# Instructions of five engines, put into the program with and without a block around them

## The chip, the cores and the metric

The kernel runs on one core of one Trainium2 chip. The metric is the device time in microseconds of one execution; the time of before is the median of three runs. A core has five engines that run on their own and meet only at semaphores: TensorE (PE; its weight loads are shown apart as PEld), VectorE (DVE), ScalarE (ACT), GpSimd (POOL) and SyncE (SP), which here only issues DMAs and waits. A name with a q behind it (SPq, PEldq) is the engine's instruction queue: rows of waits, drains, branches and DMA issues.

## The reference

For a tensor x of 2048 rows of 640 values, layer-normalised to xn, the sum of three things is computed: x itself, a spectral filter of xn and a small dense network on xn.

```python
def reference(A_x, A_w_r, A_w_i, B_x, B_w1, B_b1, B_w2, B_b2):
    x = A_x
    xn = _layernorm(x, axis=-1)
    # A: rfft2 of xn, times (w_r + 1j * w_i), irfft2
    # B: gelu(xn @ w1 + b1) @ w2 + b2, with w1 640 x 1536 and w2 1536 x 640
    return x + _A_ref(xn, A_w_r, A_w_i) + _B_ref(xn, B_w1, B_b1, B_w2, B_b2)
```

All tensors are bf16. B_x is not used.

## The kernel before

The 2048 rows lie in SBUF as 16 groups of 128 rows. The Fourier transforms are matmuls with tables that the program holds as constants (G and H for the long axis, E and GE for the short one, M and N for the small inner steps), with folds and unfolds on VectorE around them. The dense network runs on TensorE beside them: the first layer in six blocks of row groups and 12 feature blocks each, with GELU on ScalarE; the second layer and the last step of the inverse transform add up in the same PSUM banks. The last addition (line 961, on VectorE) reads a PSUM bank and the sum of x and b2, and writes an output tile; SP stores it to DRAM at line 964, 18 stores in all.

The kernel doesn't call the engines in the order of the text. Each step is put down as an operation with what it reads and writes (class Sched). The table ORDER has the fixed order of operations for each engine. `schedule` gives out the buffers, `sync` works out which waits are needed, and `emit` puts the instructions into the program: for every operation of an engine, first its waits (`wait_ge`, line 434), then the instruction itself, with a semaphore increment where somebody waits for it. SP, at the end of its list, waits for all stores (`last`, line 442), so that the kernel doesn't end before its output has landed.

Three lines matter for the change. Line 989 is where the program object is made; what the program does ahead of the kernel's own first instruction (constants, a first meeting of all engines) is shown with this line in the profile. Line 428 opens a block, entered into the `ExitStack` of line 493; lines 444 to 448 give it one body for each engine. The block is closed where that `with` statement ends, and what the closing puts into the program is shown in the profile with line 493.

Of the kernel before, what the change touches and what calls it, by code (L numbers as in the profile page):

```python
# [220 lines left out]
class Sched:  # L221
# [6 lines left out]
    def op(self, engs, prio, emit, reads=(), writes=(), after=(), rows=None, gate=(), alts=None, late=0.0):  # L228
        o = Op()
        o.name = writes[0].name if writes else ""  # L230
        o.engs, o.prio, o.emit = engs, prio, emit
        o.reads, o.writes, o.after = list(reads), list(writes), list(after)
        o.gate = gate if isinstance(gate, list) else list(gate)
        o.rows, o.late = rows, late
        o.nbytes = rows is not None
        o.alts, o.alt = alts, None
        o.seq = len(self.ops)
        o.eng, o.done, o.inc, o.count, o.sem = None, False, False, None, None
        o.deps = [w for b in o.reads for w in b.writers] + list(after)
        for b in o.reads:  # L240
            b.readers.append(o)
        for b in o.writes:
            b.writers.append(o)
        self.ops.append(o)
        return o
# [171 lines left out]
    def emit(self, es, last):  # L417
        nc = self.nc
        sems = {e: nc.alloc_semaphore(f"s_{e}") for e in self.engines if e != "sp"}
        for e in self.engines:  # L420
            n = 0
            for o in self.order[e]:
                if o.nbytes:
                    o.sem, o.count = nc.alloc_semaphore(f"d_{o.seq}"), 16
                elif o.inc:
                    n += 1
                    o.sem, o.count = sems[e], n
        block = es.enter_context(nc.Block())

        def run(name):  # L430
            def go(e):
                for o in self.order[name]:
                    for d in o.waits:
                        e.wait_ge(d.sem, d.count)
                    ins = o.emit(e, name) if o.alts is None else o.emit(e, o.alt)
                    if o.nbytes:
                        ins.then_inc(o.sem, 16)
                    elif o.inc:
                        ins.then_inc(o.sem, 1)
                if name == "sp":  # L440
                    for o in last:
                        e.wait_ge(o.sem, o.count)
            return go
        block.sync(run("sp"))
        block.gpsimd(run("pool"))
        block.vector(run("dve"))
        block.scalar(run("act"))
        block.tensor(run("pe"))


BLOCKS = [(0, 2), (2, 2), (4, 2), (6, 2), (8, 4), (12, 4)]
# [552 lines left out]
```

## Time and profile before

| | us |
|---|---|
| median of 3 runs | 147.75 (147.56 to 147.98) |
| the profiled execution's own time | 148.03 |
| its span, first to last instruction | 146.1 |
| TensorE busy in it | 140.2 |
| VectorE busy | 112.7 |
| ScalarE busy | 80.9 |
| GpSimd busy | 23.7 |

The span is measured from the start of the first recorded instruction to the end of the last; the execution's own time is longer, as it also has what lies before and behind. Waits, drains, branches and DMA issues are not counted as busy. In a view by line, a row has the line, the engine's queue, the operation, a count, the shortest, median and longest duration in nanoseconds, and the first and last start in microseconds from the span's start, printed to a tenth. The granted TensorE clock is 1.0 over the whole span.

### The profile page before, as it was taken

The numbers are of one execution on the slowest core, as the hardware profiler recorded it, in microseconds if no ns is written. First come the engines' busy times: TensorE is split into PE (matmuls) and PEld (weight loads), VectorE is DVE, ScalarE is ACT, GpSimd is POOL, SyncE is SP. The second block draws the span as 40 slices with busy tenths as digits, with TensorE's granted clock in tenths as the row PEclk, the third lists the DMA queues.
The fourth block names the chain that finished last, engine by engine and source line by source line (L and its number), as shares of the span: only waits on it lengthen the run. The fifth ranks groups of instructions, "written<-read, shape, count | busy, mean of one in ns | idle before, by whom it ended". The sixth has DMA issues, their size and how long they took to land.

```text
span 146.1 us, 4081 instructions
## 1 busy us (share of the span) xinstructions
PE 140.2 (96%) x1702; PEld 90.8 (62%) x1720; DVE 112.7 (77%) x235; ACT 80.9 (55%) x145; POOL 23.7 (16%) x40
## 2 busy tenths in 40 slices
PE   7999999999999999999999999999999999999993
PEld 7788998888465455446544645554446666556572
DVE  1999999999844449789966967992422998998982
ACT  3208999999989769763555633216376755201000
POOL 2330302206100009220100120000063700000000
PEclk9999999999999999999999999999999999999999
DMA  4999999999997875949446571444559885103234
GB/s 110 320 407 354 320 132 303 150 182 241 283 162 149 193 192 123 235 99 180 94 92 121 63 154 30 40 110 94 90 116 230 175 202 180 45 4 137 90 135 135
DMA packets 30873, 23.63 MB, mean 162 GB/s; under 512 B 20488, under 2 KB 26888, under 8 KB 30728
## 3 DMA queue, kind: packets, MB, share of 16 engines
q1 hardware_dynamic: 28432, 17.81, 52.4%
q0 software_dynamic: 2368, 5.57, 17.4%
q8 instruction: 13, 0.21, 0.6%
q14 instruction: 4, 0.03, 0.1%
q10 hardware_dynamic: 56, 0.01, 0.0%
HBM read 13.55 MB, written 2.62 MB: 111 GB/s over the span
## 4 chain that ended last, share of the span: by engine, by line
PE 91%; DVE 4%; issue 2%; DMA 2%; POOL 0%
PE ps L552 90%; DVE stats L674 2%; DMA X<-in_A_x_dram 2%; DVE T L699 1%; DVE mv L676 0%; DVE xnT L564 0%; POOL rstd L678 0%; PE ps L718 0%; DVE W L961 0%
## 5 line engine op out<-in xcount | busy, mean ns | idle before, releaser
L552 PE MATMUL ps<-xnT,W 128*128 128x256 bf16 (+2 forms) x384 | 58.7, 300 | 0.2 <-DVE mv L676 0.2
L552 PE MATMUL ps<-W,gT 128*128 128x512 bf16 (+3 forms) x380 | 55.7, 292 | 1.6 <-issue 1.1
L552 PEld LDWEIGHTS ps<-W,gT 128*128 128x128 bf16 x396 | 30.3, 98 | 23.5 <-issue 1.6
L552 PEld LDWEIGHTS ps<-xnT,W 128*128 128x128 bf16 x384 | 33.3, 98 | 16.3 <-issue 1.6
L778 ACT ACTIVATE gT<-ps,b1col 128x256 bf16<-128x256 f32 (+1 forms) x72 | 35.3, 557 | 6.8 <-PE ps L552 6.5
L674 DVE BATCH_NORM_STATS2 stats<-X 128x6 f32<-128x320 bf16 x32 | 13.9, 475 | 2.2 <-DMA X<-in_A_x_dram 2.2
L563 ACT ACTIVATE Wf<-ps 128x960 bf16<-128x960 f32 (+1 forms) x8 | 7.0, 901 | 13.5 <-PE ps L552 13.5
L946 POOL DMA_DIRECT2D X<-in_A_x_dram x8 | 7.1, 1067 | 40.1 <-DMA Wf<-in_A_w_r_dram 17.6
L845 DVE TENSOR_TENSOR T<-Y,Wf 128x1288 bf16<-128x1288 bf16 x16 | 12.7, 826 | 0.0
L946 POOL DMA_DIRECT2D xnT<-in_A_x_dram x8 | 7.4, 1151 | 25.3 <-ACT xnT L928 25.3
L678 POOL TENSOR_TENSOR rstd<-mv,mhalf 128x2 f32<-128x2 f32 (+1 forms) x10 | 7.2, 715 | 26.8 <-DVE mv L676 26.7
L563 ACT ACTIVATE Xb<-ps 128x960 bf16<-128x960 f32 (+1 forms) x7 | 7.7, 1102 | 6.8 <-PE ps L552 6.8
L564 DVE CAST Y<-ps 128x644 bf16<-128x644 f32 x8 | 6.5, 828 | 5.5 <-PE ps L552 5.5
L563 ACT ACTIVATE XV<-ps 128x1280 bf16<-128x1280 f32 (+3 forms) x10 | 9.5, 961 | 0.7 <-PE ps L552 0.7
L564 DVE CAST Xb<-ps 128x960 bf16<-128x960 f32 (+1 forms) x5 | 5.9, 1176 | 4.1 <-PE ps L552 4.1
L734 DVE TENSOR_TENSOR T<-T 128x512 bf16<-128x512 bf16 (+1 forms) x32 | 8.5, 311 | 0.0
L699 DVE TENSOR_SCALAR T<-X,mv,rstd 128x640 bf16<-128x640 bf16 (+2 forms) x17 | 7.1, 430 | 0.9 <-POOL rstd L678 0.6
L900 DVE TENSOR_TENSOR Wf<-Wf 128x960 bf16<-128x960 bf16 (+1 forms) x12 | 7.0, 597 | 0.5 <-ACT Wf L563 0.3
L961 DVE TENSOR_TENSOR W<-ps,X 128x640 bf16<-128x640 f32 x8 | 6.5, 820 | 1.1 <-PE ps L552 1.1
L849 DVE TENSOR_TENSOR Z<-T 128x644 bf16<-128x644 bf16 x16 | 7.1, 487 | 0.1
L961 DVE TENSOR_TENSOR W<-ps,xnT 128x640 bf16<-128x640 f32 (+2 forms) x10 | 6.7, 685 | 0.7 <-PE ps L552 0.7
L552 PE MATMUL ps<-etab,XV 32*128 32x160 bf16 (+1 forms) x128 | 7.2, 232 | 0.0
(55 smaller groups left out, 132.3 us busy)
## 6 DMA issues: line engine op xcount, KB each, us to landing
X<-in_A_x_dram POOLq DMA_DIRECT2D x8, 320.0 KB, 4.8
xnT<-in_A_x_dram POOLq DMA_DIRECT2D x8, 320.0 KB, 5.0
out_dram<-W SPq DMA_DIRECT2D x15, 160.0 KB, 1.8
X<-in_A_x_dram SPq DMA_DIRECT2D x7, 320.0 KB, 7.5
W<-in_B_w_dram SPq DMA_DIRECT2D x5, 384.0 KB, 6.1
W<-in_B_w_dram SPq DMA_DIRECT2D x4, 480.0 KB, 7.5
Wf<-in_A_w_i_dram SPq DMA_DIRECT2D x6, 160.5 KB, 5.8
Wf<-in_A_w_r_dram SPq DMA_DIRECT2D x6, 160.5 KB, 4.1
```

The lines of the kernel that those rows point to most:

```text
L552: ins = e.matmul(o_, lhsT=lw, rhs=rh, start=st, stop=sp_, skip_group_check=True)
L563: return e.activation(dst(), src(), ACT.Copy, scale=scale)
L564: return e.tensor_copy(dst(), src())
L674: st_op[c] = K.op([("dve", 0.393)], pr, lambda e, _, c=c, h=h: e.bn_stats(stats[:, c, 6 * h:6 * h + 6], view(X, c * D + H2 * h, [[1, H2]]) ...
L678: K.op([("pool", 0.65)], 500, lambda e, _, a=a, b=b: e.tensor_tensor(out=rstd[:, a:b], in0=mv[:, a:b, 1], in1=mhalf[:, a:b], op=ALU.pow), ...
L699: o = K.op([("dve", 0.066 + (d1 - d0) / 1980.0)], pr, lambda e, _, c=c, n=n, xnv=xnv, d0=d0, d1=d1: e.tensor_scalar(out=xnv(n, d0, [[1, d1 ...
L734: ring_ops.append(K.op([("dve", dve_us(4 * w, 2))], pr, lambda e, _, op=op, x1v=x1v, xfv=xfv, o_=o_, o0=o0, o1=o1, w=w: e.tensor_tensor(ou ...
L778: K.op([("act", act_us(128 * nt, 1))], pr + PRIO["gelu"] + GP[bi], lambda e, _, c0=c0, nt=nt, fc=fc, hps=hps, at=at: e.activation(gT[:, fc ...
L845: filt_ops.append(K.op([("dve", dve_us(4 * KP, 2))], pr, lambda e, _, k=k, Y=Y, TB=TB, pair=pair: e.tensor_tensor(out=view(TT, TB.slot * 8 ...
L849: K.op([("dve", dve_us(2 * KP, 2))], pr, lambda e, _, TB=TB, Z=Z, r=r, op=op: e.tensor_tensor(out=view(Zb, Z.slot * 4 * KP + r * KP, [[2 * ...
L946: xo_ops[c] = K.op([("pool", 0.9)], 51 - c / 20, lambda e, _, c=c, xov=xov: e.dma_start(xov(0, D), xv[:, c, :], accum_op=ALU.add), reads=[ ...
L961: K.op([("dve", dve_us(w))], 95, lambda e, _, os_=os_, fps=fps, o0=o0, w=w, xov=xov, base=base: e.tensor_tensor(out=view(W1, OST + os_.slo ...
```

## The change

The block is not opened. The same five functions are called with the program's engine objects in its place, in the same order, so each engine gets the same instructions, waits and semaphores, straight into the program that was begun at line 989.

```diff
-        block = es.enter_context(nc.Block())
 
         def run(name):
             def go(e):
@@
             return go
-        block.sync(run("sp"))
-        block.gpsimd(run("pool"))
-        block.vector(run("dve"))
-        block.scalar(run("act"))
-        block.tensor(run("pe"))
+        run("sp")(nc.sync)
+        run("pool")(nc.gpsimd)
+        run("dve")(nc.vector)
+        run("act")(nc.scalar)
+        run("pe")(nc.tensor)
```

## The prediction

> **What bounds the kernel now.** The page comes first, for the span, the busiest engine and the chain that ended last.
>
> ```profile
> span 146.1 us, 4081 instructions
> PE 140.2 (96%) x1702; PEld 90.8 (62%) x1720; DVE 112.7 (77%) x235; ACT 80.9 (55%) x145; POOL 23.7 (16%) x40
> ...
> q8 instruction: 13, 0.21, 0.6%
> ...
> PE 91%; DVE 4%; issue 2%; DMA 2%; POOL 0%
> ```
>
> TensorE is busy for 96% of the span and carries 91% of the chain that ended last. Whatever speeds up another engine in the middle of the kernel is worth nothing; a change pays only where it takes time from TensorE's stream, or before its first useful matmul, or after its last. So the two ends are read next, in the timeline and the chain:
>
> ```profile
> 0.74 0.07 issue
> 0.81 2.34 DMA X<-in_A_x_dram
> ...
> 143.14 1.28 SPq L964 DMA_DIRECT2D out_dram<-W  x3
> ...
> 143.31 0.23 PE L552 MATMUL ps<-Wf,htab 128*128 128x160 bf16 x1
> 143.58 0.32 DVE L961 TENSOR_TENSOR W<-ps,xnT 128x160 bf16<-128x160 f32 x1 [0.24 <-PE ps L552]
> ```
>
> At the start, the first load goes out at 0.81 us, 0.07 us after the engines are let go. At the end, the last matmul runs from 143.31 to 143.54, the last addition from 143.58 to 143.90, and SP issues the last three stores between 143.14 and 144.42. The compute is over at 143.9 us, and 2.2 us of the span come after it. What fills them stands in the views by line, first of the store (L964) and of the waits that SP makes for all stores (L442), asked for the stretch from 145.5 us:
>
> ```profile
> L964 SPq DMA_DIRECT2D out_dram<-W x18: 332/334/453, 120.1 to 144.0; - x18
> DMA to landing us min/median/max: 1.6/1.8/2.1
> ...
> L442 SPq EVENT_SEMAPHORE  x1: 28/28/28, 145.6 to 145.6; - x1
> ```
>
> The last store is issued at 144.0 and takes at least 1.6 us to land, which gives 145.6, and there SP's last full wait row stands. None of that is in the diff. Behind it comes L493, the line on which the `with` statement closes and with it the block:
>
> ```profile
> L493 POOLq EVENT_SEMAPHORE  x2: 17/17/17, 145.9 to 145.9; - x2
> L493 POOLq DRAIN  x1: 6442/6442/6442, 115.2 to 115.2; - x1
> L493 ACTq DRAIN  x1: 732/732/732, 134.0 to 134.0; - x1
> L493 PEldq DRAIN  x1: 1702/1702/1702, 141.9 to 141.9; - x1
> L493 DVEq DRAIN  x1: 361/361/361, 143.6 to 143.6; - x1
> L493 SPq COMPARE_BRANCH  x1: 41/41/41, 145.7 to 145.7; - x1
> L493 SPq DRAIN  x1: 7/7/7, 145.8 to 145.8; - x1
> L493 SPq EVENT_SEMAPHORE  x1: 17/17/17, 146.0 to 146.0; - x1
> L493 ACTq EVENT_SEMAPHORE  x1: 17/17/17, 146.0 to 146.0; - x1
> L493 DVEq EVENT_SEMAPHORE  x1: 21/21/21, 146.0 to 146.0; - x1
> L493 PEldq EVENT_SEMAPHORE  x1: 51/51/51, 146.0 to 146.0; - x1
> ```
>
> This is what the block costs, in the trace's own rows (engine, operation, count, duration in ns, first and last start in us). Every engine drains; the drains of POOL, ACT, PE and DVE end at 121.6, 134.7, 143.6 and 144.0 and then those engines stand and wait. SP comes last, branches to the block's end at 145.7 and drains at 145.8; POOL counts the four and releases them at 145.9; each leaves at 146.0, TensorE's row ending the span at 146.05.
>
> **The change, part by part.** The entry comes first. The same barrier stands at the start of the program, at the line on which the program object is made, outside the block:
>
> ```profile
> L989 POOLq EVENT_SEMAPHORE  x2: 17/17/17, 0.6 to 0.7; - x2
> ...
> L989 POOLq DRAIN  x1: 188/188/188, 0.4 to 0.4; - x1
> ...
> L989 SPq EVENT_SEMAPHORE  x1: 17/17/17, 0.7 to 0.7; - x1
> ...
> L989 PEldq EVENT_SEMAPHORE  x1: 51/51/51, 0.7 to 0.7; - x1
> ```
>
> It belongs to L989 and stays. No branch row stands at either line at the start; the only branch of the trace at these lines is SP's at 145.7. So the entry of the block costs nothing now, and its removal takes nothing from the first 0.81 us. Bounds for it: 0 to 0.07 us, the "issue" piece at 0.74, which is all the time between the release and the first load that could hide something of the block. I take 0, since no row of the block lies in it.
>
> The body comes second: same instructions, same order on each engine, same semaphores and waits. SP's queue, POOL's queue and TensorE's stream carry what they carried, so every term between 0.81 and 145.6 us is 0. What could still move is where the instructions lie in memory, which is the slower rival below.
>
> The closing waits come third. SP waits for 18 stores, in rows that carry up to two waits each, and one of those waits can ride on the branch. It has to stay in some form: a row like L442's, 28 ns, in the place of the branch of 41 ns. That makes a difference of 0.01 us, inside what is left of the branch's own row.
>
> The exit comes fourth. With the block go one branch (SP, 41 ns), five drains and six semaphore rows. Four of the drains are over by 144.0 and lie beside SP's wait for the stores; taking them away gains nothing by itself. On the path lie SP's branch, SP's drain, POOL's two rows, and the release with TensorE's row: 41 + 7 + 17 + 17 + 51 = 133 ns of rows, and the handovers between them. The whole of it is 146.05 − 145.7 = 0.35 us, and since starts are printed to a tenth, 0.30 to 0.40 us. Nothing is late behind it: the stores have landed, and all other engines are done 1.7 us or more before. The new last row is SP's wait, and the new span about 146.05 − 0.35 = 145.7 us.
>
> The time outside the span comes fifth. The profiled execution took 148.03 us, so 1.93 us lie before its first or behind its last instruction, and no row shows them. Before, all five engines leave the barrier together at 146.0 and go into whatever closes the run together. After, POOL, ACT, PE and DVE get there from 121.6 to 144.0 on, and SP alone is late. If closing the run takes SP's path only, this changes nothing (0). If some of it is a meeting of the five engines, the part that the early four have done by then comes off too. The nearest row for such a meeting is the block's own barrier, 0.35 us, so the bounds are 0 and 0.35 us. Below nothing is excluded for this term as long as the run only ends after its last engine, since none of the five gets there later. I take 0.1: TensorE leaves the barrier last (51 ns against 17 of SP), and a part of the handovers is made ahead, but SP, the latest, still has to do its own share.
>
> The sum for the profiled execution is 148.03 − 0.35 − 0.10 = 147.58 us. That execution was 0.28 us over the median of the three timed runs (147.75, from 147.56 to 147.98), so in the terms of the median the forecast is 147.75 − 0.45 = 147.3 us. About 0.3%, 0.44 us, is what a measurement of this kernel can tell from no change; the forecast lies on that line, and the chances below show it.
>
> The Trainium skill speaks to the fifth term: "Runtime: NRT & Kernel Launch", in the breakdown of preamble and postamble, has the runtime put a barrier of its own behind every kernel, some 1.5 us, in which it waits until all engines are done. No row here shows that barrier. By its figure, if the early four engines could walk all of it before SP comes, the time would be 147.75 − 0.35 − 1.5 = 145.9 us, an estimate from that page; I don't follow it, as SP must be waited for in any such barrier.
>
> **The rivals.** First, nothing is gained (147.75 us; from 147.6 to 147.9). The L989 rows show that a barrier can stand in this program without any block. If the end of a program gets one in the same way, or the run's end waits as long for the engines as the block did, the rows change their line and the time stays. For it speaks that the 1.93 us outside the span must hold some ending; against it that no barrier row besides those of L989 and L493 is in the trace.
>
> Second, the gain is double: the run's close is a meeting of the five engines of the same price, and the early four have done their share. Then 0.35 + 0.35 us go: 147.05 us. For it speaks that POOL, ACT, PE and DVE stand idle for 1.7 us and more at L493; against it that the latest engine still has to take its own steps.
>
> Third, slower: the instructions move in memory. TensorE's stream is fetched in blocks while it runs: the row of q8 has 13 fetches that took 0.6% of 16 engines' span, 0.006 × 16 × 146.1 / 13 = 1.08 us each. Now they are hidden, as the view of waits shows for TensorE:
>
> ```profile
> PE ps L552 <- issue: 1.3, 8, 0.2
> ```
>
> Eight pauses that nothing visible explains, the longest 0.2 us, so none of the 13 fetches stops TensorE for its 1.08 us. If, without the block, the engines' code is laid out so that a fetch starts too late, each one exposed costs up to 1.08 us less what it hides now. A single one in full gives 147.75 − 0.35 + 1.08 = 148.5 us; it decides from the point at which more than 0.35 + 0.44 = 0.8 us of a fetch is exposed. Against it speaks that the branch goes at the end of SP's stream alone and TensorE's keeps its order, losing only a drain and a semaphore row at its end; for it only that the layout of the program isn't shown in a trace.
>
> **How the numbers follow.** Forecast (the exit's 0.35 us go, and 0 to 0.2 us beside): 0.60, own range 147.1 to 147.45; half of it and a little more lies beyond 0.3%, at 147.31 or below. Nothing gained: 0.14. Double gain: 0.15. Slower: 0.11. So faster by over 0.3% gets 0.35 + 0.15 = 0.50, within 0.3% gets 0.25 + 0.14 = 0.39, slower 0.11. The range has to hold 8 in 10: from 146.85 (the double gain's 147.05 less the 0.2 us by which the lowest of the three runs lies under the median) to 147.75 (nothing gained); outside are the slower rival and a part of both ends.
>
> **What would show it.** In the profile after: no row of L493, no drain at the end of any engine, and as last row of the span an SP wait at 145.6 to 145.7; a span of 145.65 to 145.75 us. The L989 rows and the first load at 0.81 us stay as they are, the last addition still starts at 143.58 within 0.1 us, and TensorE's longest "issue" pause stays at 0.2 us. The profiled execution's own time less its span falls from 1.93 us to between 1.58 and 1.93; a value over 1.93 would show that the run's end has taken over the wait, which is the first rival. The forecast is wrong if a barrier row remains at the end, if TensorE's last matmul ends elsewhere than at 143.5 us (then the body has moved), or if the span falls by 0.35 us and the time doesn't.

## The result and the profile after

The kernel without the block takes 147.01 us in the median where before takes 147.94 in the same comparison; the ratio is 0.9941, with a 95% interval of 0.9921 to 0.9961. A second comparison, on another occasion, gave 0.9924 (0.9893 to 0.9954). That is 0.9 to 1.1 us, two to two and a half times the 0.45 us that were forecast; the time lies inside the forecast range.

The profile doesn't look like a gain at first. The page of after, and its view by line of SP's waits and of the stores (one `block = ...` line is gone, so all line numbers behind it are smaller by one):

```profile
span 146.7 us, 4087 instructions
PE 141.6 (97%) x1720; PEld 90.0 (61%) x1720; DVE 112.6 (77%) x235; ACT 81.4 (55%) x145; POOL 23.7 (16%) x40
...
L963 SPq DMA_DIRECT2D out_dram<-W x18: 332/334/452, 121.1 to 145.0; - x18
...
L441 SPq EVENT_SEMAPHORE  x9: 27/28/28, 145.5 to 146.6; - x9
```

The span is 0.6 us longer than in the profile of before, not 0.35 us shorter. The closing part is as predicted: nothing stands behind SP's ninth wait row, there is no drain and no meeting of the engines at the end, and the span ends with that wait. The start is the same too: the meeting at the line of the program object (now L988) and the first load at 0.81 us. What is longer is the stretch between, which the change doesn't touch. The last store goes out at 145.0 instead of 144.0. The timeline's last matmul, and TensorE's pauses in the view of waits, say the same:

```profile
144.34 0.23 PE L551 MATMUL ps<-Wf,htab 128*128 128x160 bf16 x1
...
PE ps L717 <- DVE T L698: 0.9, 1, 0.9
PE ps L551 <- DVE T L733: 0.9, 2, 0.7
```

TensorE waited 0.9 us for VectorE at the first transposes (0.3 us in before) and 0.9 us more, in two pieces, at a fold. VectorE in turn waited longer for rows of x, as the views of waits show, after first, then before:

```profile
DVE stats L673 <- DMA X<-in_A_x_dram: 5.0, 3, 2.4
```

```profile
DVE stats L674 <- DMA X<-in_A_x_dram: 2.2, 1, 2.2
```

So in this execution the loads landed late, and TensorE ended 1.03 us later (144.57 against 143.54).

One difference between the two pages is none of the kernels. Each lists 1720 weight loads, but before's has only 1702 matmuls: 18 of its matmul records are missing. The rows of one kind of matmul, before first, then after, show where most of them went:

```profile
L552 PE MATMUL ps<-W,gT 128*128 128x512 bf16 (+3 forms) x380 | 55.7, 292 | 1.6 <-issue 1.1
```

```profile
L551 PE MATMUL ps<-W,gT 128*128 128x512 bf16 (+3 forms) x396 | 58.7, 295 | 0.0
```

The eight "issue" pauses of TensorE that the prediction read in before are holes left by missing records: where all 396 are there, the row has no such pause. TensorE's busy time of 140.2 us in before is too small for the same reason. The second profile of after also has 1702 matmuls, and 4069 instructions, which is before's 4081 less the exit's twelve rows.

Is the later end the change or the execution? The comparisons made for the experiments below recorded each execution with its span, so it can be counted. Before, 94 executions: span 145.3 to 147.6, median 145.9. After, 33 executions: 144.9 to 147.0, median 145.7 (one more, at 148.87 us, counts as slow and is left out). Both scatter by about 2 us; the profiled execution of after is one of its longer ones. One profile of each would have read the difference the wrong way round.

The time outside the span, in contrast, hardly scatters (spans are recorded to a tenth of a microsecond, so some 0.1 us of the ranges is rounding):

| | executions | outside the span, median (lowest to highest), us |
|---|---|---|
| before | 94 | 2.01 (1.84 to 2.15) |
| after | 33 | 1.26 (1.21 to 1.31) |

So 0.75 us of the gain lie outside the span, where no row of a profile stands. Inside it, where the exit's rows stood, the traces give a number without the scatter of the body: from the landing of the last store to the end of the span pass 0.47 us in both profiles of before and 0.04 us in both of after, which is 0.43 us less. Together that is 1.18 us. The medians of the times over the same executions, 147.88 and 146.95, differ by only 0.93, since the medians of the spans differ by 0.2 us; the missing 0.2 us are within the scatter of the body.

The experiments are about the 0.75 us. No record says how the time outside the span is split between its two ends; as the start of the program is the same, its differences are put down to the end. Theory A: all engines go through a close of their own behind the kernel's last row, and with the block gone four of them do so early. Theory B: the engines' streams are shorter by some instructions, and the close needs one fetch of instructions less (the DMA packets of before's trace have one of 8 KB 1.8 us behind the span's end, after's have none). Theory C: the body moved.

### The profile page after: what moved, and what is told of

It is laid out like the page before. It is cut to its first block, busy times and chain, and to the rows that moved or that the text cites. A ratio compares the mean times of both kernels' runs of the same rounds, so it can differ in the third digit from the quotient of the medians.

```text
span 146.7 us, 4087 instructions
## 1 busy us (share of the span) xinstructions
PE 141.6 (97%) x1720; PEld 90.0 (61%) x1720; DVE 112.6 (77%) x235; ACT 81.4 (55%) x145; POOL 23.7 (16%) x40
## 4 chain that ended last, share of the span: by engine, by line
PE 74%; DVE 12%; DMA 9%; SPq 2%; issue 1%; POOL 1%
PE ps L551 74%; DMA X<-in_A_x_dram 9%; DVE stats L673 5%; DVE T L733 3%; DVE T L729 2%; SPq L546 1%; DVE T L698 1%; POOL rstd L677 1%; DVE mv L675 1%; SPq L705 0%; DVE W L960 0%; DVE xnT L563 0%
## 5 line engine op out<-in xcount | busy, mean ns | idle before, releaser
L551 PE MATMUL ps<-W,gT 128*128 128x512 bf16 (+3 forms) x396 | 58.7, 295 | 0.0
```

What stands on the lines that cost most here:

```text
L551: ins = e.matmul(o_, lhsT=lw, rhs=rh, start=st, stop=sp_, skip_group_check=True)
```

## Experiments

The first run is before, unchanged; all edits that follow are made to the kernel after.

**Before once more**, unchanged, for the spans of single executions.

> The kernel of before, unchanged, so that each of its executions has its span beside its time. Theory A (the time outside the span shrank because four engines now reach the close of the run early) and theory B (it shrank because the engines' streams are shorter by some instructions, so that the close needs no further block of instructions fetched: before has a fetch of 8 KB 1.8 us behind the span, after has none) both expect 1.9 to 2.0 us outside the span in every execution, spans around 146.0 and a ratio of 1.000. Theory C (the stretch up to the last store itself moved with the change) expects the spans of before, less the 0.35 us of the closing barrier, to differ from the spans of after by more than their scatter.

Ratio 1.001 (0.9981 to 1.0039); outside the span 2.03 us (1.88 to 2.15), spans 145.4 to 147.1, median 145.8. The profiled execution had a span of 146.6, and TensorE's waits in it:

```profile
PE ps L552 <- issue: 1.3, 8, 0.2
...
PE ps L552 <- DVE X L952: 0.7, 1, 0.7
PE ps L718 <- DVE T L699: 0.7, 1, 0.7
```

The pause at the first transposes, 0.7 us here and 0.3 in the first profile, comes and goes in before too, and in after's second profile it is 0.2 us. Theory C isn't needed: the scatter of the body belongs to both kernels. Whether the body's median also moved by some 0.2 us can't be told within that scatter.

**The meeting alone, without a block.**

```diff
         run("pe")(nc.tensor)
+        nc.all_engine_barrier()
```

> After, with the meeting of all five engines put back at the end, without a block. Theory A: everything comes back, 1.9 to 2.0 us outside the span, span as before (0.35 us more than after), ratio 0.998 to 1.002. Theory B: only the span's 0.35 us come back, since no branch and no labels are added; 1.25 us outside, ratio near 0.9965. If the block's entry were the cause, nothing but 0.35 us would come back either.

Ratio 0.9994 (0.9974 to 1.0014), outside 2.06 us (1.91 to 2.12), median span 145.65. The time is back; outside the span this run and the one before it lie 0.06 and 0.03 us over the 1.9 to 2.0 expected. The view by line shows rows as those of L493 again, under the new line:

```profile
L448 POOLq EVENT_SEMAPHORE  x2: 17/17/17, 145.5 to 145.6; - x2
L448 POOLq DRAIN  x1: 6471/6471/6471, 115.0 to 115.0; - x1
...
L448 SPq DRAIN  x1: 13/13/13, 145.5 to 145.5; - x1
...
L448 PEldq EVENT_SEMAPHORE  x1: 51/51/51, 145.7 to 145.7; - x1
```

There is no branch among them. In the traces of before, SP's drain starts 0.21 us behind the end of its last wait row (both profiles), and here 0.04 us behind it: so the branch cost SP 0.17 us, and the exit's 0.47 us are 0.30 here. In the ratio, whose interval is 0.4% wide, that can't be seen. Nearly all that the block cost is the meeting at its exit; its entry has no row in before, and no cost that the ratio shows.

**Late without meeting.** POOL, DVE, ACT and PE each wait for the last store, as SP does.

```diff
         run("pe")(nc.tensor)
+        for e in (nc.gpsimd, nc.vector, nc.scalar, nc.tensor):
+            e.wait_ge(last[-1].sem, last[-1].count)
```

> After, with POOL, DVE, ACT and PE each waiting for the last store as SP does: no drains, no meeting, but all five leave together. Theory A: the time outside the span is back at 1.9 to 2.0 us while the span stays short, so the time is 0.3 to 0.4 us under before (ratio 0.997 to 0.998). Theory B: each stream is one instruction longer only, 1.25 us outside, ratio as after, 0.993 to 0.995.

Ratio 0.9979 (0.9957 to 1.0002); outside 1.91 us (1.87 to 1.96). The end of the profile has no drain and no exchange, only five waits that end together:

```profile
L441 SPq EVENT_SEMAPHORE  x9: 27/28/28, 145.1 to 146.2; - x9
...
L449 ACTq EVENT_SEMAPHORE  x1: 17/17/17, 146.2 to 146.2; - x1
L449 POOLq EVENT_SEMAPHORE  x1: 17/17/17, 146.2 to 146.2; - x1
L449 DVEq EVENT_SEMAPHORE  x1: 21/21/21, 146.2 to 146.2; - x1
L449 PEldq EVENT_SEMAPHORE  x1: 51/51/51, 146.2 to 146.2; - x1
```

Being late is enough: 0.65 of the 0.75 us are back with one wait for each engine. Theory B is out, since here, too, no fetch stands behind the span, and yet the time is there. (Before's fetch also ends 2.29 us behind the span, and the execution's own time of 148.03 us leaves no more than 1.98 us behind it.) What the other 0.1 us are isn't shown; the drains of the next run are a candidate.

**Drains without meeting.**

```diff
         run("pe")(nc.tensor)
+        for e in (nc.sync, nc.gpsimd, nc.vector, nc.scalar, nc.tensor):
+            e.drain()
```

> After, with a drain at the end of each engine and no semaphore between them. Theory A: four of the five drain early, so as after: 1.25 us outside, ratio 0.993 to 0.995; only SP's drain of 7 ns lies on the path. If the drains themselves were the cost, the ratio would be near 1.

Ratio 0.9964 (0.9937 to 0.9991); outside 1.44 us (1.39 to 1.48), where 1.25 was expected. Rows by line:

```profile
L449 POOLq DRAIN  x1: 8113/8113/8113, 115.7 to 115.7; - x1
L449 ACTq DRAIN  x1: 732/732/732, 134.5 to 134.5; - x1
L449 PEldq DRAIN  x1: 1702/1702/1702, 142.5 to 142.5; - x1
L449 DVEq DRAIN  x1: 364/364/364, 144.2 to 144.2; - x1
L449 SPq DRAIN  x1: 7/7/7, 146.2 to 146.2; - x1
```

Four drains are early, as expected. SP's, the only late one, is the span's last row, 7 ns long, and yet the execution ends 0.18 us later behind it than behind a wait. I had priced it by its row; that was wrong. No run has SP's drain without the other four; that it alone makes the 0.18 us is likely, but not shown. Most of the 0.75 us isn't drains, though.

**Which engine must not be late.** The wait for the 18 stores is moved from SP to one other engine, so that this one alone is late.

```diff
-                if name == "sp":
+                if name == "pool":      # and "dve", "act", "pe"
                     for o in last:
                         e.wait_ge(o.sem, o.count)
```

> After, with the wait for the 18 stores moved from SP to POOL: POOL alone is late, the other four reach the close of the run by 145 us at the latest. Measured is the time outside the span: 1.26 us in after (SP alone late), 1.91 with all five late. Theory A1 (each engine has its own way to go from its last instruction to the end of the run, and the longest that starts last sets it): one of the four engines moved to shows 1.8 to 1.95 us, the others less; for POOL, which counts the others in the kernel's own meeting, I expect 1.3 to 1.9. Theory A2 (a cost for each late engine, some 0.16 us): 1.2 to 1.3 us.

> After, with the wait for the 18 stores moved from SP to DVE. Theory A1: its own way, anywhere from 1.0 to 1.95 us outside the span. Theory A2: 1.2 to 1.3 us as for SP.

> After, with the wait for the 18 stores moved from SP to ACT. Theory A1: its own way, anywhere from 1.0 to 1.95 us outside the span. Theory A2: 1.2 to 1.3 us as for SP.

> After, with the wait for the 18 stores moved from SP to PE, whose semaphore row is the slowest (51 ns against 17). Theory A1: the likeliest to carry the 1.8 to 1.95 us outside the span. Theory A2: 1.2 to 1.4 us.

| late alone | outside the span, us | ratio to before, each in its own comparison |
|---|---|---|
| SP (after) | 1.26 (1.21 to 1.31) | 0.9941 (0.9921 to 0.9961) |
| DVE | 1.35 (1.32 to 1.39) | 0.9901 (0.9867 to 0.9936) |
| ACT | 1.40 (1.37 to 1.43) | 0.9949 (0.9919 to 0.9978) |
| PE | 1.57 (1.51 to 1.58) | 0.9914 (0.9877 to 0.9952) |
| POOL | 1.77 (1.72 to 1.83) | 0.9951 (0.9919 to 0.9983) |

The views by line show that the last row is that engine's wait in place of SP's, POOL's here and then DVE's:

```profile
L441 POOLq EVENT_SEMAPHORE  x3: 43/43/43, 145.0 to 145.5; - x3
```

```profile
L441 DVEq EVENT_SEMAPHORE  x1: 50/50/50, 145.3 to 145.3; - x1
```

Each engine has a way of its own to the end of the run, from 1.26 us (SP) to 1.77 (POOL); what lies ahead of the first row is in each of these numbers. A price for each late engine (A2) is out: it gave 1.2 to 1.3 us, for PE up to 1.4, and DVE, ACT, PE and POOL all lie above. A1 fits in kind, though its longest way, 1.77 us, falls just short of the 1.8 to 1.95 expected. It was POOL and not PE that carried the longest. The ratios also hold the scatter of the body, over 5 to 10 executions each, so the DVE version's 0.9901 is no proof that it beats after; its time outside is 0.09 us longer.

**POOL late beside SP, and POOL alone early.**

```diff
         run("pe")(nc.tensor)
+        for e in (nc.gpsimd,):                        # the first
+        for e in (nc.vector, nc.scalar, nc.tensor):   # the second
+            e.wait_ge(last[-1].sem, last[-1].count)
```

These are two versions; each has one of the two `for` lines and the wait under it.

> After, with POOL alone waiting for the last store besides SP; DVE, ACT and PE go early. Outside the span were 1.26 us with SP alone late, 1.77 with POOL alone late, 1.91 with all five. If the longest way that starts last sets it, POOL's way carries nearly all: 1.75 to 1.9 us. If the late ones add up (SP and POOL two of five), 1.4 to 1.5.

> After, with DVE, ACT and PE waiting for the last store besides SP; POOL alone goes early. If the longest way sets it, PE's 1.57 us do: 1.55 to 1.7. If the late ones add up, four of five: 1.7 to 1.8.

With POOL and SP late, 1.93 us (1.90 to 1.97), ratio 0.9958 (0.9933 to 0.9983): as much as with all five (1.91). With all but POOL late, 1.54 us (1.52 to 1.57), ratio 0.9919 (0.9885 to 0.9952): as much as PE alone (1.57). Both miss the numbers expected of the longest way (1.75 to 1.9 and 1.55 to 1.7) by 0.03 and 0.01 us, and those of a sum (1.4 to 1.5 and 1.7 to 1.8) by 0.43 and 0.16. The rows of the two, in the views by line:

```profile
L449 POOLq EVENT_SEMAPHORE  x1: 17/17/17, 145.6 to 145.6; - x1
```

```profile
L449 ACTq EVENT_SEMAPHORE  x1: 17/17/17, 145.2 to 145.2; - x1
L449 DVEq EVENT_SEMAPHORE  x1: 21/21/21, 145.2 to 145.2; - x1
L449 PEldq EVENT_SEMAPHORE  x1: 51/51/51, 145.2 to 145.2; - x1
```

One wait row of 17 ns on POOL costs 0.67 us of time, and three waits on three other engines cost 0.28. So the longest way among the late engines sets most of the end; their ways don't add up. It isn't the whole account: by it alone POOL with SP would give 1.77 us and not 1.93. That 0.16 us is open. POOL's last row is 43 ns long where it is late alone and 17 here, which explains 0.03 of it at most. A fetch doesn't explain it: the trace with POOL late alone has a packet of 8 KB 0.18 us behind the span, and the one with POOL and SP, the longer of the two, has none.

**After once more**, beside these two.

> The kernel after, unchanged, on the same chip as the two before it. Outside the span 1.22 to 1.31 us as found, the shortest span 0.3 to 0.4 us under the shortest of before, ratio 0.992 to 0.996.

Ratio 0.9924 (0.9893 to 0.9954), outside 1.25 us (1.21 to 1.31), shortest span 144.9 against 145.5 of before in the same comparison. This 0.6 us difference is more than the 0.3 to 0.4 expected; with 12 and 24 executions it may be scatter, which no run here settles.

## Why the prediction was right, and where it was off

**The direction and the place were right.** The chain ends in SP's wait for the last store, and what stood behind it was the exit; it is gone and nothing came in its place. The rival that nothing is gained fell with the wait row that ended the span and with the ratio, and the meeting without a block showed what the time would have been: before's.

**The entry was right at 0.** The first load goes out at 0.81 us in both profiles, and the meeting without a block, which has no entry, costs what the block cost within the ratio's interval.

**The exit's term was a little small.** 0.35 us were forecast, 0.30 to 0.40 as bounds, and 0.43 us went by the traces' rows. The rows that went are the ones named. The step that was off is the closing waits: a wait row was expected in the place of SP's branch. The view by line of before has nine wait rows for the 18 stores, as many as after:

```profile
L442 SPq EVENT_SEMAPHORE  x9: 17/28/28, 144.5 to 145.6; - x9
```

So the branch went without a replacement, and the span ends with the ninth row, as before's would have without the exit. From the end of that row to the end of the branch are 0.08 us in the trace of before: that is what the term lacks.

**The body stayed, but the test for it was bad.** I had written that the forecast is wrong if the last matmul ends elsewhere than at 143.5 us. It ended at 144.57, so by its own words the forecast was wrong there. But the same matmul ends at 144.07 in before's second profile, and between 143.17 and 144.69 in other profiles without a block, so the place of one end says little about the change. The test needed the scatter over several executions, which one profile can't show.

**The term outside the span was mis-sized.** It was forecast at 0.1 us, between 0 and 0.35, and measured 0.75. This is the step that failed, and most of the gain lies in it. Its reasoning had two parts. That an early engine can do its share ahead was right. That the block's own meeting, 0.35 us, is the upper bound for such a share was wrong: it bounded a time without rows by a row of another thing. The share that counts is the difference between the longest way to the end, POOL's 1.93 us when late with SP, and SP's 1.26: 0.67 of the 0.75 us. No row of before stood for either. "SP, the latest, still has to do its own share" was right, and SP's share is the shortest of the five. I named TensorE for the part made ahead, by its row of 51 ns; the engine that sets it is POOL, and TensorE would have been next, with 1.57. (The 1.93 us that the prediction starts from are 1.98 by the span's finer end of 146.05, which it uses elsewhere; that changes nothing.)

**The rivals.** The double gain gave 147.05 us, nearer to the 147.01 measured than the forecast's 147.3. That nearness is partly luck: by the gain, its 0.70 us fall short of the 0.93 and 1.12 measured, as before's median was 147.94 in this comparison and not 147.75. It was right that the early four engines do a share ahead, and wrong on the price: 0.75 us and not the 0.35 of the block's meeting. The slower rival didn't come: no pause of TensorE for a fetch is to be seen. Its "issue" pauses are gone from after's first profile, which has all matmul records, and in the second, which lacks 18, they are what they were in before:

```profile
PE ps L551 <- issue: 1.3, 8, 0.2
```

The page "Runtime: NRT & Kernel Launch" of the Trainium skill (breakdown of preamble and postamble), with its barrier of 1.5 us that waits for all engines, agrees in kind: whichever engine ends last, 1.26 us or more lie outside the span, and how much depends on that engine. The runs don't split that time into stages, nor into what lies ahead of the span and behind it, so no run here shows the figure itself, and the 145.9 us worked out from it were not reached.

## What to carry to other kernels

On this kernel the end of the last engine isn't the end of the execution: look at each execution's time less its span, and at which engines are held until then. Let the engine that has to wait for the last store be the one with the shortest way out (here SP), let all others, POOL above all, run out of work early, and don't make them meet at the end when one engine's wait already guards the output. Compare spans over many executions before reading a difference of 1 us in the body out of two profiles, and count the matmul records against the weight loads before reading a pause of TensorE.

## What the runs showed of the hardware

I hadn't expected that the time behind the last row depends so much on the engine that ends last: 1.26 us for SP, 1.35 for DVE, 1.40 for ACT, 1.57 for PE and 1.77 to 1.93 for POOL, each steady to about 0.1 us, with what lies ahead of the span counted in. Nor that with drains at the end, of which only SP's is late and has a row of 7 ns, the execution ends 0.18 us later (1.44 against 1.26), or that a branch whose row is 41 ns holds SP up by 0.17 us.
